# A two-layer H3/MLP training step on one core: four edits to the order of transfers and of one normalisation

## The chip, the core and the metric

The kernel runs on one core of a Trainium2 chip. A core has five engines with queues of their own: TensorE (PE: matmuls; PEld is its loading of weights), VectorE (DVE), ScalarE (ACT), GpSimd (POOL) and SyncE (SP), which issues transfers and does no arithmetic. Transfers (DMAs) are issued by SyncE, ScalarE or GpSimd and carried out by 16 DMA engines that all of these share. [...] The metric is the time of one execution on the device, in microseconds (us), less is better.

## The reference

The program computes a forward pass through four residual blocks and all gradients of it. With S = 2048 positions, D = 448 features and F = 1792 hidden units:

```
x  = A_q
x += A(layernorm(x));  x += B(layernorm(x))      # layer 0
x += A(layernorm(x));  x += B(layernorm(x))      # layer 1

A(q) = q * (irfft(rfft(kv) * rfft(ssm_k)) + kv * ssm_D)
       kv = (k convolved with a filter of 4 taps) * v
B(x) = silu(x @ w1) @ w2
outputs: x, and the gradients for A_q, A_k, A_v, A_shift_k, A_ssm_k, A_ssm_D, B_w1, B_w2
```

The long convolution does not depend on x, so both layers share its result Y. The backward pass of a B block needs, for each position and hidden unit, the slope of silu at the pre-activation, and products of activations and gradients over all positions for the gradients of w1 and w2.

## The kernel before, in words

The program is one Python function that is traced from top to bottom. A planner then puts each engine's instructions in an order of its own: by the order of tracing as a priority, by when it reckons that an instruction's inputs are ready, and by when a buffer comes free. Two calls bind it. `issue_after(x)` puts what is traced inside it behind instruction x on x's engine (order alone, no wait for x to finish); `keep_in_program_order` puts an instruction behind everything traced earlier on its engine. A tile belongs to a pool and a tag, and a tag has a number of buffers; a new tile of a tag can be written only when the oldest one's readers have finished.

The work has these stages, with the times at which they run in the profile of before:

1. **Prefix** (`_ssm_prefix`, 0 to 98 us). It loads k, v, ssm_k and the constants, transposes, and does the long convolution as Fourier transforms made of matmuls. The spectrum of ssm_k is called Ka (in tile Z), the spectrum of kv comes out of A1kv and lies in tile A1K. The loop over two halves h and four groups i does, per step: the short convolution (`conv`, L383), stage 1 of the previous group (`stage1_kv`, L399), in the first half a transposition of a part of Ka's input (`turn`, L365), in the second half two chunks of stage 2 of Ka (`_fft_stage2`, L221, evicted by `cons_ka`). In steps 2 and 3 of the first half `_ln` also normalises the first chunk of positions (tile x0c in, tile na out; ACT L278, DVE L264 to L273). After each two chunks of Ka's spectrum, GpSimd stores them to DRAM (`spec_K`, L413); and it copies them into KB with the two halves of the partitions swapped (`_swap_halves_dma`, L249 and L250). Then stage 2 of kv runs chunk by chunk in `cons_prod`: ScalarE or VectorE evicts the spectrum, GpSimd stores it after each two chunks (`spec_KV`, L448), and VectorE multiplies it by Ka (pa, L451) and by KB (pb, L452) for the inverse transform. The stored spectra are read back in stage 5.
2. **Forward of both layers** (98 to 373 us, `Main.run`, interleaved with layer 1's backward pass). Positions are in four chunks c of 512. `h` multiplies by w1 (tile w1sb, L537) and stores the activations turned (`store_turned`: two transposing DMAs, L503, into the one buffer `turned`, and later a plain store, L504) and, for layer 0, the pre-activations (`DT_d`, L645). `out` multiplies by w2 (tile w2sb). Both weights are loaded right behind the prefix in the tracing (L186 to L189), into the buffers of the prefix's M1sb and v_n.
3. **Backward of layer 1** (228 to 412 us): `ga` multiplies the incoming gradient by w2 transposed (ps_g) and by the slopes (ghT), `gn` multiplies by w1 transposed (ps_n, L740) and goes back through the normalisations on ScalarE and VectorE.
4. **Backward of layer 0** (395 to 517 us): the same with the stored pre-activations, loaded by `load_d` (L769, tile dTl) one chunk ahead and turned into slopes by ScalarE (L614). In `ga`, at steps 3 and 6 of 7, the next half of dTl is loaded, and then a finished half of ghT is turned and stored: for half 0 by `store_turned`, which first issues a store still pending from the half before (`flush`), for half 1 by a plain store (L507). `x_turn` (L674) turns the next chunk's gradient. Jobs of the w2 gradient (`_job`: 16 matmuls ps_d, L904, with an operand tile dstat loaded by L902 or, with transposition, by L900) fill PE in between.
5. **Suffix** (517 to 737 us, `_ssm_suffix`): the backward Fourier transforms, with the jobs of the w2 gradient and then of the w1 gradient (`_gw1`) woven between. `_gw1` makes 14 blocks ft of 128 columns, each of two jobs. ScalarE evicts a block (dout, L966); the first 12 blocks are turned by a transposing DMA (tile do, L941) and stored by two plain DMAs (L933, L934). `store` stores the blocks already turned, and `turn(ft)` is called in the first job of block ft + 1.

The lines that place the store of a turned block and the load of a derivative half:

```
def turn(ft, o):
    if ft < NF - 2:
        store()
        o7 = pool.tile([P, ND, P], BF16, name="do7", tag="do7", bufs=2)
        nc.sync.dma_start_transpose(out=o7[:], in_=o[:])
...
if loads[hh]:
    ld.append(self.load_d(*loads[hh]))
if L == 1 or hh == 0:
    self.store_turned(k.GH_d[L], ghT[hh], c, hh)
```

## Time and profile before

| | |
|---|---|
| median of three runs | 739.4 us (737.02 to 741.23) |
| the profiled execution | 738.77 us, of which the span from the first to the last instruction 736.6 us |
| granted TensorE clock, mean | 0.992 |
| PE, DVE, ACT, POOL busy | 94%, 69%, 58%, 9% of the span |
| bytes moved by DMA | 180.11 MB, mean 245 GB/s |
| issued by SyncE and ScalarE (hardware_dynamic) | 156.34 MB |
| issued by GpSimd (software_dynamic) | 22.65 MB |

A line of the timeline has the start and the duration in us, the engine (SPq: SyncE's queue), the line of the kernel, the operation, the tile written and the tiles read, the number of instructions merged, and in brackets how long the engine stood idle before and what ended that. A transfer's line is the time of its issue; when it lands is another matter. In the rows of 40 slices a digit is the busy share in tenths, 9 for 90% or more.

### The profile page before, as it was taken

How to read it: one execution, taken by the hardware profiler on the slowest of the kernel's cores; microseconds unless marked ns; L12 is line 12 of the kernel's file. 1: busy time of each engine (PE TensorE's matmuls, PEld its weight loads, DVE VectorE, ACT ScalarE, POOL GpSimd, SP SyncE). 2: the span in 40 equal slices, each digit the busy share in tenths (PEclk: the TensorE clock that was granted, in tenths of full speed). 3: DMA queues.
4: the chain of work that ended last, by engine and by line, in shares of the span. 5: the costliest groups of instructions: out<-in, count | busy, mean ns of one | idle time of the engine just before them, and what ended most of it. 6: DMA issues, size and time to landing. Idle time of an engine off the chain costs nothing. (4 is left out here: it accounts for less than half of the span.)

```text
span 736.6 us, 12192 instructions
## 1 busy us (share of the span) xinstructions
PE 690.3 (94%) x4753; PEld 362.6 (49%) x4753; DVE 507.6 (69%) x1059; ACT 424.1 (58%) x539; POOL 62.7 (9%) x111
## 2 busy tenths in 40 slices
PE   6988789999999998999999799999999999999987
PEld 5766533443344443443444334445465767755533
DVE  4878888787743597895958788798224777199423
ACT  4688877766437577487576476763723666531101
POOL 1143221111100002000000000000000000000000
PEclk9999999999999999999999989999999999999999
DMA  9979969999875878979999999997799999899966
GB/s 311 240 179 277 354 212 319 280 290 281 244 153 143 202 158 208 188 205 200 239 223 289 185 348 263 255 270 257 268 252 215 297 322 348 279 275 243 208 144 154
DMA packets 234789, 180.11 MB, mean 245 GB/s; under 512 B 179178, under 2 KB 215598, under 8 KB 233580
## 3 DMA queue, kind: packets, MB, share of 16 engines
q1 hardware_dynamic: 228238, 156.34, 82.4%
q0 software_dynamic: 5872, 22.65, 9.0%
q8 instruction: 37, 0.61, 0.4%
q10 hardware_dynamic: 622, 0.35, 0.3%
q14 instruction: 20, 0.16, 0.1%
HBM read 69.58 MB, written 63.77 MB: 181 GB/s over the span
## 5 line engine op out<-in xcount | busy, mean ns | idle before, releaser
L904 PEld LDWEIGHTS <-dstat 128*128 128x128 bf16 x896 | 85.1, 98 | 80.8 <-DMA dstat<-GP_d 4.4
L537 PE MATMUL ps_h<-nT,w1sb 128*128 128x512 bf16 (+1 forms) x448 | 102.1, 381 | 6.8 <-DVE dT L113 5.2
L537 PE MATMUL ps_g<-gT,w2T 128*128 128x512 bf16 (+1 forms) x448 | 96.0, 381 | 3.2 <-ACT ghp L690 3.1
L740 PE MATMUL ps_n<-w1T,ghT 128*128 128x448 bf16 x448 | 92.6, 360 | 5.0 <-ACT lb_u L742 3.6
L904 PE MATMUL ps_d<-mov,dstat 128*128 128x448 bf16 x448 | 89.5, 352 | 3.5 <-DMA dstat<-GP_d 3.5
L629 ACT ACTIVATE aT<-ps_h 128x1024 bf16<-128x1024 f32 (+1 forms) x64 | 58.4, 916 | 55.2 <-PE ps_h L537 38.3
L658 PE MATMUL ps_o<-w2sb,aT 128*128 128x448 bf16 x448 | 90.1, 353 | 0.0
L113 DVE CAST dT<-ps_h 128x1024 bf16<-128x1024 f32 (+1 forms) x55 | 58.3, 1063 | 27.8 <-ACT aT L629 27.8
L537 PEld LDWEIGHTS <-w1sb 128*128 128x128 bf16 (+1 forms) x448 | 35.9, 96 | 69.7 <-issue 41.2
L740 PEld LDWEIGHTS <-ghT 128*128 128x128 bf16 x448 | 43.5, 99 | 48.6 <-issue 7.7
L537 PEld LDWEIGHTS <-w2T 128*128 128x128 bf16 (+1 forms) x448 | 35.4, 96 | 61.9 <-issue 29.2
L690 ACT CAST ghp<-ps_g 128x1024 bf16<-128x1024 f32 x56 | 55.4, 1007 | 17.1 <-PE ps_g L537 13.1
L658 PEld LDWEIGHTS <-aT 128*128 128x128 bf16 x448 | 42.4, 98 | 42.3 <-issue 3.6
L904 PE MATMUL ps_d<-X,dstat 128*128 128x448 bf16 x224 | 52.2, 353 | 0.0
L904 PE MATMUL ps_d<-GO,dstat 128*128 128x448 bf16 x224 | 50.2, 353 | 0.0
L742 ACT ACTIVATE lb_u<-ps_n,rstd 128x448 f32<-128x448 f32 x32 | 20.2, 633 | 37.0 <-DVE X L727 17.7
L966 ACT CAST dout<-ps_d 128x448 bf16<-128x448 f32 x14 | 7.5, 534 | 51.8 <-PE ps_d L904 43.9
L233 PEld LDWEIGHTS <-pb 128*128 128x128 bf16 x336 | 32.5, 98 | 9.1 <-DVE pb L452 5.7
L614 ACT ACTIVATE dTl<-dTl 128x1024 bf16<-128x1024 bf16 (+1 forms) x32 | 29.8, 944 | 12.0 <-DMA dTl<-DT_d 12.0
L232 PEld LDWEIGHTS <-pa 128*128 128x128 bf16 x336 | 32.8, 98 | 7.2 <-DVE pa L451 4.3
L698 DVE TENSOR_TENSOR ghT<-dT,ghp 128x1024 bf16<-128x1024 bf16 (+1 forms) x32 | 19.8, 621 | 20.4 <-ACT ghp L690 20.3
L659 DVE TENSOR_TENSOR X<-X,ps_o 128x448 bf16<-128x448 bf16 x32 | 19.7, 615 | 16.3 <-PE ps_o L658 16.2
(188 smaller groups left out, 1091.7 us busy)
## 6 DMA issues: line engine op xcount, KB each, us to landing
A_d<-turned SPq DMA_DIRECT2D x12, 896.0 KB, 4.6
GH_d<-turned SPq DMA_DIRECT2D x12, 896.0 KB, 5.1
dstat<-A_d SPq DMA_DIRECT2D x21, 512.0 KB, 5.0
dstat<-GH_d SPq DMA_DIRECT2D x21, 512.0 KB, 4.7
DT_d<-dT SPq DMA_DIRECT2D x8, 896.0 KB, 6.5
dTl<-DT_d SPq DMA_DIRECT2D x8, 896.0 KB, 6.6
spec_K<-Z POOLq DMA_DIRECT2D x7, 512.0 KB, 7.5
KB<-Z POOLq DMA_DIRECT2D x14, 256.0 KB, 12.5
```

The costliest lines, as they stand in the source:

```text
L113: eng.tensor_copy(out, in_)
L232: nc.tensor.matmul(o, lhsT=pa[:, i * P:(i + 1) * P], rhs=k.Gsb[:, ga, :], start=True, stop=False)
L233: nc.tensor.matmul(o, lhsT=pb[:, i * P:(i + 1) * P], rhs=k.Gsb[:, gb, :], start=False, stop=True)
L537: self.nc.tensor.matmul(o, lhsT=w[lo:hi, b, f:f + P], rhs=r, start=(seen[u] == 1), stop=(seen[u] == ND))
L614: self.k.last_slope = self.nc.scalar.activation(s, s, ACT.Derivative_silu)
L629: last = nc.scalar.activation(a, ps[:, 0:n, :], ACT.Silu)
L658: nc.tensor.matmul(po[:, :D], lhsT=aT[ft // 7][0][:, ft % 7, tl * P:(tl + 1) * P], rhs=self.w2sb[:, ft, :], start=(ft == 0), stop=(ft == N ...
L690: k.last_gh = nc.scalar.copy(gh[:], ps[:])
L698: nc.vector.tensor_tensor(out=ghT[hh][:, o:o + len(u), :], in0=dT[hh][1][:, o:o + len(u), :], in1=gh[:, u[0]:u[0] + len(u), :], op=ALU.mult)
L740: mm = nc.tensor.matmul(pn[:, :D], lhsT=ghT[ft // 7][:, ft % 7, tl * P:(tl + 1) * P], rhs=self.w1T[:, ft, :], start=(ft == 0), stop=(ft == ...
L742: last_u = nc.scalar.activation(u0[:], pn[:, :D], ACT.Identity, scale=k.rstd[2 * L + 1][:, t:t + 1], accum_out=cp[:, tl, 0:1])
L904: i = k.nc.tensor.matmul(ps[:, :D], lhsT=st[:, t, :], rhs=mov[:, t, :], start=start and t == 0, stop=stop and t == NT - 1)
```

## The change

Four things are edited, and no arithmetic is:

- In `_gw1`, `turn` issues the transposing DMA of its block first and the stores of the block before it behind that.
- In `ga`, for layer 0 and where a derivative half is loaded, the pending store and both transposing DMAs of `store_turned` are put behind that load.
- In the prefix, the stores of both spectra are issued by SyncE and no longer by GpSimd. The loads of w1 and w2 are traced inside the prefix, ahead of the last three pairs of Ka's chunks.
- In the prefix, the first chunk's normalisation is traced in steps 0 and 1 of the first half and not in steps 2 and 3.

```
     _ssm_prefix(k)
-    k.w1sb = k.wk.tile([P, ND, F], BF16, name="w1sb", tag="WA")
-    nc.sync.dma_start(out=k.w1sb[:, 0:3, :], in_=k.B_w1[0:384].rearrange("(c p) f -> p c f", p=P))
-    nc.sync.dma_start(out=k.w1sb[:, 3, :], in_=k.B_w1[320:448])
-    k.w2sb = k.wk.tile([P, NF, D], BF16, name="w2sb", tag="WB")
-    nc.sync.dma_start(out=k.w2sb[:], in_=k.B_w2.rearrange("(c p) d -> p c d", p=P))
...
-                nc.gpsimd.dma_start(out=k.SPEC_d["K"][:, lo:hi], in_=Ka[:, lo:hi])
+                nc.sync.dma_start(out=k.SPEC_d["K"][:, lo:hi], in_=Ka[:, lo:hi])
...
-                if 4 * h + i in (2, 3):
-                    _ln(k, work, 0, lambda tl: k.x0c0[:, tl, :], 0, k.na0, ((2 * i - 4, 2 * i - 2),), pin=True, store=i == 3)
+                if 4 * h + i in (0, 1):
+                    _ln(k, work, 0, lambda tl: k.x0c0[:, tl, :], 0, k.na0, ((2 * i, 2 * i + 2),), pin=True, store=i == 1)
...
         stage1_kv(*prev)
+        k.w1sb = k.wk.tile([P, ND, F], BF16, name="w1sb", tag="WA")
+        nc.sync.dma_start(out=k.w1sb[:, 0:3, :], in_=k.B_w1[0:384].rearrange("(c p) f -> p c f", p=P))
+        nc.sync.dma_start(out=k.w1sb[:, 3, :], in_=k.B_w1[320:448])
+        k.w2sb = k.wk.tile([P, NF, D], BF16, name="w2sb", tag="WB")
+        nc.sync.dma_start(out=k.w2sb[:], in_=k.B_w2.rearrange("(c p) d -> p c d", p=P))
...
-                nc.gpsimd.dma_start(out=k.SPEC_d["KV"][:, (ci - 1) * 1024:(ci + 1) * 1024], in_=Zf[:, (ci - 1) * 1024:(ci + 1) * 1024])
+                nc.sync.dma_start(out=k.SPEC_d["KV"][:, (ci - 1) * 1024:(ci + 1) * 1024], in_=Zf[:, (ci - 1) * 1024:(ci + 1) * 1024])
...
                 if L == 1 or hh == 0:
-                    self.store_turned(k.GH_d[L], ghT[hh], c, hh)
+                    with self.tc.issue_after(k.d_load.ins) if L == 0 and loads[hh] else ExitStack():
+                        self.store_turned(k.GH_d[L], ghT[hh], c, hh)
...
         if ft < NF - 2:
-            store()
             o7 = pool.tile([P, ND, P], BF16, name="do7", tag="do7", bufs=2)
-            nc.sync.dma_start_transpose(out=o7[:], in_=o[:])
+            with k.tc.issue_after(nc.sync.dma_start_transpose(out=o7[:], in_=o[:]).ins):
+                store()
```

## The prediction

> **What bounds the kernel now.** I read the page first: TensorE (PE) is the bound.

> ```profile
> PE 690.3 (94%) x4753; PEld 362.6 (49%) x4753; DVE 507.6 (69%) x1059; ACT 424.1 (58%) x539; POOL 62.7 (9%) x111
> DMA  9979969999875878979999999997799999899966
> ```

> PE is free for only 46.3 us of the 736.6 us span, and the DMA engines are nearly full for most of it. So an edit gains only where it closes a hole in PE or a stretch at half clock. I therefore went through the timeline in windows, looked for those holes near the edited lines, and then asked the view of waits who ended each. There are four places.

> *Place 1, the end of the w1 gradient.* SyncE's queue (SPq), then PE, both from the timeline (start, duration, ..., idle before and who ended it):

> ```profile
> 695.95 1.22 SPq L941 DMA_TRANSPOSE do<-dout  x1
> 701.94 0.40 SPq L933 DMA_DIRECT2D out_dram<-do  x1
> 703.00 2.26 SPq L900 DMA_TRANSPOSE dstat<-GP_d  x1
> ...
> 707.58 6.23 PE L904 MATMUL ps_d<-mov,dstat 128*128 128x448 bf16 x32 [1.36 <-DMA dstat<-GP_d]
> 715.97 10.77 PE L904 MATMUL ps_d<-mov,dstat 128*128 128x448 bf16 x56 [2.16 <-DMA dstat<-GP_d]
> ```

> The planner put the store of a turned block (L933) right behind that block's own transpose (L941). SyncE stands still from 697.17 to 701.94 until the transpose lands, the load of the next operand stands behind it, and PE starves twice: 1.36 + 2.16 = 3.5 us.

> *Place 2, the first chunk of the layer-0 backward pass.* SyncE, ScalarE and PE:

> ```profile
> 410.37 2.83 SPq L503 DMA_TRANSPOSE turned<-ghT  x1
> 413.24 0.58 SPq L769 DMA_DIRECT2D dTl<-DT_d  x1
> ...
> 421.23 1.06 ACT L614 ACTIVATE dTl<-dTl 128x1024 bf16<-128x1024 bf16 x1 [7.37 <-DMA dTl<-DT_d]
> ...
> 416.15 2.81 PE L740 MATMUL ps_n<-w1T,ghT 128*128 128x448 bf16 x14
> 422.95 5.38 PE L740 MATMUL ps_n<-w1T,ghT 128*128 128x448 bf16 x14 [3.61 <-ACT lb_u L742]
> ```

> The derivative input is issued behind a transpose and lands at 413.24 + 8.0. ScalarE waits 7.37 us for it, with the reading of a PSUM bank queued behind. PE idles 3.61 us, and then runs the same 14 matmuls in 5.38 instead of 2.81 us, because the clock has dropped. Together 3.61 + 2.57 = 6.2 us.

> *Place 3, the prefix, where the first chunk's normalisation stands.*

> ```profile
> 36.83 1.74 PE L383 MATMUL ps_cv<-KB 112*128 112x112 bf16 x32
> 39.17 1.03 PE L221 MATMUL ps_s<-Z,Gsb 128*128 128x512 bf16 x4
> 42.37 2.97 PE L383 MATMUL ps_cv<-KB 112*128 112x112 bf16 x32 [2.17 <-ACT A1kv L111]
> 46.33 1.03 PE L221 MATMUL ps_s<-Z,Gsb 128*128 128x512 bf16 x4
> ...
> 40.06 1.41 ACT L278 ACTIVATE na<-x0c,ln_nmr,rstd 128x448 bf16<-128x448 bf16 x2 [0.50 <-DVE ln_nmr L273]
> ```

> From one set of stage-2 matmuls to the next it is 46.33 - 39.17 = 7.2 us; the next two steps take 3.4 us each (49.70, 53.10). ScalarE does the normalisation (1.41 us, again at 43.19) ahead of the evictions that PE waits for, and after the hole the convolution takes 2.97 instead of 1.74 us. Excess: 3.8 us.

> *Place 4, the swapped spectrum KB.*

> ```profile
> 71.89 0.57 POOL L413 DMA_DIRECT2D spec_K<-Z  x1 [0.85 <-DMA KB<-Z]
> 75.50 0.52 POOL L250 DMA_DIRECT2D KB<-Z  x1 [1.25 <-DMA KB<-Z]
> ...
> 84.75 0.69 DVE L452 TENSOR_TENSOR pb<-A1K,KB 128x1024 bf16<-128x1024 bf16 x1 [1.76 <-DMA KB<-Z]
> ```

> From 64 us on each transfer of GpSimd (POOL) starts just as the one eight places ahead of it lands, so the stores of the spectrum take places from the swaps. VectorE, busy for nearly all of 68 to 82 us, then stands 1.76 us for a swap that was issued at 70.53 and took 14.0 us.

> [...] at 42.37 a hole of 2.17 us was enough, and the 2.16 us hole at 713.8 was not, so I count the clock only where the trace shows it.

> **The change part by part.**

> *Stores of w1 blocks.* The transpose of block n+1 now precedes the store of block n, whose own transpose is then some 6 us old (two jobs of 16 matmuls, 3.03 us each), against landing times of 2.5 to 7.6 us. Nothing is added: same 12 transposes and 24 stores. SyncE loses its waits there (21.7 us over 9 stores), and the operand load for 707.58 can issue at about 697.2, landing with its 4.5 us at 702, 4 us ahead of need. Bounds: 0 (if SyncE's issue time of 5 to 7 us per 6.06 us pair of jobs binds by itself) to 3.5. I take 3.5, since the slots come free four jobs ahead. Next late would be a transpose waiting for the store two blocks back; that store has 6 us to land in.

> *Derivative inputs.* Three chunks, L769 ahead of two transposes (L503). In the first, the slot is free when ghT's half is done, about 407.5, so the load issues some 5.5 us sooner and lands near 413 (shortest seen 5.7 us), when ScalarE wants it. The price: the pending store of the previous turned half (405.42, 4.9 us) is queued behind the load too, and the transposes wait for its buffer. They start near 414.5, not 410.37; but the transfers up to the next gT are the same, so later landings stay about where they are. That caps the gain: grad_out (GO) lands at 429.17 + 11.8 = 441.0 for a first use at 444.83, 3.9 us of slack; the next derivative lands at 429.2 for 433.54, 4.3; VectorE's chain, which restarts at 422.94, could restart at 418.5, 4.4. So of 6.2 us I take 3.9. In the second chunk the load must wait for its slot until about 439.3 and holds back a transpose that issued at 434.39, but transfers were backed up until 441 anyway: 0. In the third it gains nothing on PE. Bounds: -2 (a transpose or GO later by the length of one load, which shows nowhere now) to 6.2.

> *Normalisation two steps sooner.* Same instructions. The excess of 3.8 us goes. The steps at 27 to 36 us, paced by PE at 3.2 us, receive 3.7 us of VectorE work (bn_stats 0.6 each and small ones) and 2.8 of ScalarE. Before each eviction there ScalarE idles 1.0 to 1.8 us and VectorE 0.8 to 1.1, so most fits; in-order queues will delay some evictions. I charge 1.2 and take 2.6. Bounds -1 to 3.8. Its input was issued at 10.20 and took 13.8 us, so it is there at 24.

> *Spectra on SyncE.* 14 issues of 0.54 us leave GpSimd, and 14 places free up. The swaps then issue several us sooner and DVE's 1.76 us goes: 1.7. Bounds 0 to 2.5 (with 0.69 at 67.45). SyncE is idle from 58.9 to 89.7, so the 14 issues cost nothing there; the spectra are first read at 524.8. Queued behind them are the x0 loads (89.74, 7.0 us to land), wanted at 102.18: if the stores back up, that slack of 5 us, shrunk by the 4.3 won, goes first.

> *w1 and w2 loads traced sooner.* They issued at 54.16 to 57.40 and were first used at 102.5. They only have to stay ahead of the stores: 0.

> Sum: 3.5 + 3.9 + 2.6 + 1.7 = 11.7. The profiled execution took 738.77 around its span of 736.6; minus 11.7 it is 727.1. The median of the runs is 739.4, 0.6 above it: **727.7 us**.

> **Rivals.**
> (a) Layer 0 is fed by the DMA engines, busy through all of 410 to 490 (share 1.06): the stall moves to GO or the next derivative. For: slacks of only about 4 us. Then 3.5 + 2.6 + 1.7: 731.6.
> (b) The prefix gains nothing: evictions now wait behind the normalisation in steps paced by PE, or x0 is late. With the other two parts in half: about 735.5.
> (c) All holes close with no new one: 3.5 + 6.2 + 3.8 + 2.5 = 16, 723.4.
> (d) Slower: the load, first in SyncE's queue, waits for its slot while transposes, stores and the next operand stand behind it, and each of the three chunks stalls as the first does now. Two new stalls of 6.2 us and the old one kept cost 12.4 against 7.8 won: 744. It decides once ScalarE's waits pass about 4 us per chunk. Against: the slot is freed by the very multiplication whose result the transposes need.
> (e) The change doesn't do what it says, because the planner times everything else anew: within 0.5%, near 738.

> **How the numbers follow.** Forecast 0.58, (a) 0.17, (b) 0.07, (c) 0.08, (d) 0.05, (e) 0.05. The likeliest case spans 724 to 731.5; with (a) and part of (c) the range is 722 to 734.5. Half a per cent (3.7 us) is about what a measurement here can tell: faster 0.88, same 0.07, slower 0.05.

> **What would show it.** Right: L933 behind the next L941 with no wait for do<-dout, and no PE hole at dstat<-GP_d; L769 ahead of both L503 and the 7.37 us wait nearly gone; no half clock near 42 or 422; no pb wait for KB. Wrong: ScalarE waiting for dTl in the second or third chunk, PE waiting for GO, holes of 1 us in steps at 27 to 36 us, or x0c late at 98.

## The result, and the profile after

The changed kernel took 728.6 us (median of four runs, 727.79 to 731.37) against 739.8 before (four runs; the first three gave 739.4): a ratio of 0.987, 95% interval 0.984 to 0.990. The forecast was 727.7. Measured again later, beside 27 executions of the kernel before, it was 729.8 (six executions) against 736.3: 0.991, interval 0.988 to 0.994. Both put the time inside the forecast range, and both intervals lie below 1; but the gain was 11 us the first time and 6.6 the second, and the difference is what the experiments had to explain.

The page of the kernel after, engines and DMA share:

```profile
PE 689.2 (95%) x4753; PEld 361.7 (50%) x4753; DVE 507.4 (70%) x1059; ACT 424.0 (58%) x539; POOL 55.0 (8%) x97
DMA  9969959999976877878989999999699898999994
```

TensorE's free time fell from 46.3 to 727.5 - 689.2 = 38.3 us, its work stayed, and GpSimd lost the 14 stores. The timeline of the same kernel at the four places (start, duration, queue or engine, ..., idle before and who ended it):

```profile
33.28 1.41 ACT L273 ACTIVATE na<-x0c,ln_nmr,rstd 128x448 bf16<-128x448 bf16 x2 [1.27 <-DVE ln_nmr L268]
...
35.53 1.73 PE L378 MATMUL ps_cv<-KB 112*128 112x112 bf16 x32 [1.19 <-ACT ks L380]
38.01 0.93 PE L394 MATMUL ps_s<-kvt,M1sb 128*128 128x224 bf16 x8 [0.74 <-DVE Z L113]
...
69.94 0.52 POOL L245 DMA_DIRECT2D KB<-Z  x1 [0.55 <-DMA KB<-Z]
...
82.25 0.69 DVE L452 TENSOR_TENSOR pb<-A1K,KB 128x1024 bf16<-128x1024 bf16 x1
...
407.48 0.32 SPq L770 DMA_DIRECT2D dTl<-DT_d  x1
...
413.71 1.04 ACT L614 ACTIVATE dTl<-dTl 128x1024 bf16<-128x1024 bf16 x1
...
419.13 2.81 PE L741 MATMUL ps_n<-w1T,ghT 128*128 128x448 bf16 x14
...
425.76 1.17 SPq L871 DMA_DIRECT2D GO<-in_grad_out_dram  x1
427.04 8.70 SPq L674 DMA_TRANSPOSE gT<-X  x1
...
700.04 17.95 PE L905 MATMUL ps_d<-mov,dstat 128*128 128x448 bf16 x94
...
700.88 1.21 SPq L941 DMA_TRANSPOSE do<-dout  x1
702.19 0.52 SPq L934 DMA_DIRECT2D out_dram<-do  x1
...
703.34 2.49 SPq L901 DMA_TRANSPOSE dstat<-GP_d  x1
```

- *The end.* The store (L934) follows the next block's transpose without a stop, the operand's load (L901) follows at once, and 94 matmuls run from 700.04 to 717.99 with no hole.
- *Layer 0, first chunk.* The derivative load (L770) goes at 407.48, ScalarE has its input at 413.71 without a wait, and the 14 matmuls that stood 3.61 us and ran 5.38 now come unbroken in 2.81.
- *Spectrum.* The last swap is issued at 69.94 (one was still to come at 75.50 before), and the pb of VectorE that waited 1.76 us before, now at 82.25, waits for nothing, like all others.
- *Prefix.* The holes at 42 us are gone, but the normalisation at 33.28 now stands ahead of ScalarE's eviction, and TensorE stands 1.19 and 0.74 us at 35 and 38.

By differences of start times between the two profiled executions: tail -3.87, last matmuls -0.37, layer 0 -5.11 and +0.29, convolution -1.24, spectrum -1.73, a later start +0.59, between the first ps_y and layer 0 +2.38, where a half-clock stretch came (granted clock 0.50 from 98.89 to 105.71 us; 1.00 there before), elsewhere -0.05; together -9.1, the difference of the spans.

### The profile page after: what moved, and what is told of

Same layout as the page of the kernel before. It is cut to its first block, busy times and chain, and to the rows that moved or that the text cites. A ratio compares the mean times of both kernels' runs of the same rounds, so it can differ in the third digit from the quotient of the medians.

```text
span 727.5 us, 12191 instructions
## 1 busy us (share of the span) xinstructions
PE 689.2 (95%) x4753; PEld 361.7 (50%) x4753; DVE 507.4 (70%) x1059; ACT 424.0 (58%) x539; POOL 55.0 (8%) x97
## 5 line engine op out<-in xcount | busy, mean ns | idle before, releaser
L537 PE MATMUL ps_h<-nT,w1sb 128*128 128x512 bf16 (+1 forms) x448 | 104.7, 389 | 6.6 <-DVE dT L113 5.1
L741 PE MATMUL ps_n<-w1T,ghT 128*128 128x448 bf16 x448 | 90.2, 353 | 2.1 <-DVE ghT L698 2.0
L614 ACT ACTIVATE dTl<-dTl 128x1024 bf16<-128x1024 bf16 (+1 forms) x32 | 29.8, 943 | 6.6 <-DMA dTl<-DT_d 6.6
```

What stands on the lines that cost most here:

```text
L537: self.nc.tensor.matmul(o, lhsT=w[lo:hi, b, f:f + P], rhs=r, start=(seen[u] == 1), stop=(seen[u] == ND))
L614: self.k.last_slope = self.nc.scalar.activation(s, s, ACT.Derivative_silu)
L741: mm = nc.tensor.matmul(pn[:, :D], lhsT=ghT[ft // 7][:, ft % 7, tl * P:(tl + 1) * P], rhs=self.w1T[:, ft, :], start=(ft == 0), stop=(ft == ...
```

## The experiments

Each was timed against the kernel before on its own chip. A single part is worth less than the spread of the runs, so I also measured stages in each trace, from the start of one set of matmuls to that of another, which keeps a gain apart from what happens elsewhere. "Convolution" runs from the first ps_cv matmul to the 225th, "spectrum" on to the first ps_y, "chunk 1" from the 253rd ps_n to the 337th, "rest of layer 0" on to the first ps_gK, "tail" from the first ps_sk to the first ps_dt.

### The four parts alone, on the kernel before

*w1 stores:*

```diff
-            store()
             o7 = pool.tile(...)
-            nc.sync.dma_start_transpose(out=o7[:], in_=o[:])
+            with k.tc.issue_after(nc.sync.dma_start_transpose(out=o7[:], in_=o[:]).ins):
+                store()
```

> The kernel before with the w1 block stores alone put behind the next block's transpose. Theory (four independent gains): the two PE holes at dstat<-GP_d, 1.36 and 2.16 us, go, and the end comes 3.5 to 3.9 us sooner, with nothing changed before 690 us. Rival (the holes closed because the earlier stages ran ahead and the DMA engines were freer by then): under 1.5 us, one of the two holes stays.

Ratio 0.9966 (0.9949 to 0.9982), medians 733.1 against 735.7, so 2.6 us, with an interval of 1.3 to 3.8. Tail: 34.66 us, in this run and in all seven others with this part 34.65 to 34.81; in the six without it 36.81 to 39.09, mean 38.02. That is 3.4 us on average, 3.9 from the profiled execution that I predicted from. The rival falls: both holes go without the earlier parts, as the timeline of this kernel shows.

```profile
706.02 17.95 PE L904 MATMUL ps_d<-mov,dstat 128*128 128x448 bf16 x94
```

*Derivative loads:*

```diff
-                    self.store_turned(k.GH_d[L], ghT[hh], c, hh)
+                    with self.tc.issue_after(k.d_load.ins) if L == 0 and loads[hh] else ExitStack():
+                        self.store_turned(k.GH_d[L], ghT[hh], c, hh)
```

> The kernel before with the layer-0 derivative loads alone put ahead of the transposes. My recorded cap: 3.9 us. Theory after the result: about 5 us, since GO and the next derivative load move up too, so the 3.61 us hole and the half clock behind it (2.57 us) both go, and 1 us comes back with a wait further on. Rival (it needs the prefix to run ahead): under 3 us.

Ratio 0.9997 (0.9976 to 1.0018): nothing. That is the rival's number, but not for its reason. The profiled execution was the longest of its 22 (741.2 us against a median of 735.9), so it is read for its places, not for its length. Chunk 1 is as after (47.57 us), so the move works alone; but the rest of layer 0 is 165.04 instead of 159.46, with a wait of TensorE for an operand (dstat<-A_d, 4.83 us) that the kernel before doesn't have. Neither theory nor cap foresaw that; "The third chunk" below follows it.

*Normalisation:*

```diff
-                if 4 * h + i in (2, 3):
-                    _ln(..., ((2 * i - 4, 2 * i - 2),), pin=True, store=i == 3)
+                if 4 * h + i in (0, 1):
+                    _ln(..., ((2 * i, 2 * i + 2),), pin=True, store=i == 1)
```

> The kernel before with the first chunk's normalisation alone moved to steps 0 and 1. Theory: 1.2 us sooner at 47 us (the 3.8 us excess goes, holes of 1.2 and 0.7 us come at 35 to 38 us), and that much or less at the end. Recorded: 2.6. Rival (a stall only changed its place): 0 to 0.5 at 47 us, or slower.

Ratio 0.9998 (0.9983 to 1.0014). The convolution takes 25.12 us, 1.24 less than before, and the spectrum stage gives it back: 42.49 instead of 41.45. VectorE of this kernel, in the timeline:

```profile
84.79 0.69 DVE L452 TENSOR_TENSOR pb<-A1K,KB 128x1024 bf16<-128x1024 bf16 x1 [2.68 <-DMA KB<-Z]
```

It arrives sooner at the same late swap and waits 2.68 instead of 1.76 us. With the swaps as they were, the normalisation's place is worth nothing that these times can tell (0.2 us at the first ps_y).

*Spectra on SyncE, w1 and w2 loads moved:*

```diff
-                nc.gpsimd.dma_start(out=k.SPEC_d["K"][:, lo:hi], in_=Ka[:, lo:hi])
+                nc.sync.dma_start(out=k.SPEC_d["K"][:, lo:hi], in_=Ka[:, lo:hi])
...
-                nc.gpsimd.dma_start(out=k.SPEC_d["KV"][:, ...], in_=Zf[:, ...])
+                nc.sync.dma_start(out=k.SPEC_d["KV"][:, ...], in_=Zf[:, ...])
```

with the five lines of the w1 and w2 loads moved into the prefix as in the change.

> The kernel before with the spectra stored by SyncE and the w1 and w2 loads moved, nothing else. Theory: VectorE's wait of 1.76 us for KB goes and the first ps_y matmul comes 1.7 us sooner, kept to the end. Rival (the prefix's end is paced by something else and the wait shows up there): 0 to 0.5.

Ratio 0.9981 (0.9962 to 1.0000). The spectrum stage takes 39.71 us, against 41.45 before: 1.7, as forecast. It is 39.71 or 39.72 in the five other profiles with this part in which the normalisation is not put on VectorE. The 0.37 us at the end comes with this part too, which nobody forecast: from the first ps_dt to the end of the span it is 9.69 to 9.71 us in the eight profiles with the spectra on SyncE and 10.06 to 10.22 in the six without. Why, no run here shows.

By their ratios the four parts alone sum to 4.3 us, and the change measured whole gives 6.6 (below). About 1 us of the difference is the normalisation, which needs the spectra moved; the rest is within the intervals.

### Does the gain hang on the execution?

The same file as the changed kernel.

> The changed kernel once more, on one chip with the next three and the kernel before. Theory: its gain does not hang on the chip, 9 to 11 us, and its executions show the half clock near 100 us again. Rival (single parts summed to only some 4 us, and each profiled execution loses a different number of half-clock windows): the gain is 5 to 8 us here, and part of the 11 measured first was the clock and the chip.

0.9911 (0.9880 to 0.9942): 6.6 us, the rival's 5 to 8. This time the profiled execution (span 725.1 us) had no half clock at all before the end (mean granted clock 0.998). The view of windows, cut into steps of 3.41 us (in the first profile 98.89 and 105.71 us, where the granted clock changed, bound two of them; columns: window, its length, TensorE busy, granted clock, DMA share, GB/s), of the kernel after, first profile:

```profile
95.48:98.89 3.41, 1.71 (x19) 1.00 0.82 330
98.89:102.30 3.41, 2.52 (x10) 0.50 0.39 148
102.30:105.71 3.41, 3.41 (x11) 0.50 0.00 0
```

and of the same kernel in its second:

```profile
94.75:98.16 3.41, 1.88 (x15) 1.00 0.92 370
98.16:101.58 3.42, 2.27 (x16) 1.00 0.40 153
101.58:104.99 3.41, 3.34 (x18) 1.00 0.01 4
```

The holes at this place are the same (1.43, 0.27 and 0.9 to 1.0 us). Only the steps fell otherwise: one step held TensorE busy for 1.71 us and the clock was halved for the next two; here the emptiest held 1.88 and it was not. What filled the step differs too: 1.14 of the 1.71 us were transposes on TensorE (matmuls with the identity, ps_t<-ident), against 0.71 of the 1.88. Over all 14 profiles the stage from the first ps_y to the 253rd ps_n takes 323.6 to 324.0 us in the five without half clock near 100 us and 325.1 to 327.2 in the nine with it, 2.4 more on average.

At the hole that place 2 was priced from, a half clock is a matter of the execution as well. Kernel before:

```profile
418.07:421.48 3.41, 1.27 (x7) 1.00 1.37 117
421.48:424.90 3.42, 1.95 (x6) 0.50 1.32 161
```

and the kernel with the normalisation alone moved, whose code there is unchanged and whose wait for lb_u was 1.33 us:

```profile
419.09:422.50 3.41, 2.63 (x14) 1.00 1.27 251
422.50:425.91 3.41, 2.85 (x16) 1.00 1.09 204
```

So chunk 1 took 52.73 us in the profile that I predicted from, but 50.42, 49.91, 49.62 and 49.55 in four other kernels with the same code, against 47.6 with the load moved (48.64 in one of nine). In that one execution ScalarE had the load late enough for a hole of 3.61 us, against 0.98 to 1.85 in the other four, and the hole left TensorE busy for only 1.27 us of one step of the clock.

### The third chunk

In the changed kernel, the load moved in the first chunk only; SyncE's order differs only in the third, where one transpose stands ahead of the load again:

```diff
-                    with self.tc.issue_after(k.d_load.ins) if L == 0 and loads[hh] else ExitStack():
+                    with self.tc.issue_after(k.d_load.ins) if L == 0 and c == 0 and loads[hh] else ExitStack():
```

> The changed kernel with the derivative load ahead of the transposes in the first layer-0 chunk only; SyncE's order differs from the changed kernel's only in the third chunk, where one transpose goes ahead of the load again. Theory: the third chunk gains nothing, and having both transposes behind the load makes the operand loads that follow late (a wait of 4.83 us for dstat<-A_d in the run with this part alone, 0.76 in the changed kernel): 0.5 to 1 us faster than the changed kernel in the median, and no wait for A_d near 505 us. Rival: the order in the third chunk does nothing, within 0.3 us of the changed kernel.

0.9900 (0.9872 to 0.9928), median 728.65 against 729.77 for the changed kernel beside it: the right direction, not separable by times. The trace is clearer: no wait for A_d; the rest of layer 0 takes 159.73 us.

The same single-chunk edit alone, on the kernel before:

> The kernel before with the derivative load ahead of the transposes in the first layer-0 chunk only. Theory: the gain of the first chunk (2 to 3 us without the clock, 5 with it) stays to the end since the late operand near 507 us does not come: 2 to 3.5 us faster than before in the median. Rival (the derivative part gains nothing on the average, since the half clock behind its hole was that one execution's): within 1 us of before, as with all three chunks.

0.9981 (0.9962 to 0.9999), 1.8 us by medians where all three chunks gave 0: just under the 2 that the theory asked for, and above the rival's 1. The two intervals overlap, so that the third chunk takes the gain back is read from the traces and from the spread: the 22 times of the kernel with all three chunks have a standard deviation of 3.3 us, against 2.2 here and 2.1 for the kernel before. Chunk 1 took 47.57 us, the rest 159.96.

Over all the traces, the rest of layer 0 takes 159.46 to 159.75 us in the five kernels with the old order everywhere, 159.71 to 159.96 in the three with only the first chunk moved, and 159.47, 159.75, 160.17, 162.30, 165.04 and 165.52 in the six with all three. So the third chunk costs nothing in some executions and 6 us in others. The loss goes with the time for which the two transposes of that chunk (L503) hold SyncE: 8.8, 11.4, 11.7, 12.6, 13.6 and 14.8 us in the six profiles, and TensorE's wait for A_d there is 0, 0.76, 1.65, 2.19, 4.83 and 4.51 us.

### The normalisation on VectorE

On the changed kernel (the four instructions are then not counted in the balance, which shifts a few later choices):

```diff
-                    _ln(..., ((2 * i, 2 * i + 2),), pin=True, store=i == 1)
+                    _ln(..., ((2 * i, 2 * i + 2),), pin=True, eng=nc.vector, store=i == 1)
```

> The changed kernel with the early normalisation's four scale-and-shift instructions on VectorE instead of where the balance put them. Theory: the new PE hole of 1.19 us at ks goes, since ScalarE's queue no longer has 1.41 us ahead of the eviction, while VectorE's 0.3 us each lengthen the wait at Z: 0.5 to 1 us sooner at the convolution's end than the changed kernel, of which what reaches the first ps_y matmul is less. Rival (the prefix's end is paced by the swaps into KB): nothing at ps_y.

0.9879 (0.9848 to 0.9911). Convolution 23.87 us instead of 25.11, and the spectrum stage 39.19 instead of 39.71, so all of it arrives: 1.8 us at ps_y, more than the 0.5 to 1 expected. The rival falls. Whether the 0.5 us of the spectrum stage is the normalisation's or that of the shifted choices isn't shown. But in the profiled execution, 4.5 us went at the third chunk. Its timeline there, SyncE's queue and TensorE:

```profile
457.03 14.77 SPq L503 DMA_TRANSPOSE turned<-ghT  x2
...
480.91 8.95 SPq L503 DMA_TRANSPOSE turned<-ghT  x2
494.41 0.53 SPq L504 DMA_DIRECT2D GH_d<-turned  x1
...
495.74 2.51 SPq L903 DMA_DIRECT2D dstat<-A_d  x2
...
503.69 1.67 PE L905 MATMUL ps_d<-GO,dstat 128*128 128x448 bf16 x4 [4.51 <-DMA dstat<-A_d]
505.16 4.59 PE L741 MATMUL ps_n<-w1T,ghT 128*128 128x448 bf16 x14
```

Both transposes behind the derivative load keep SyncE for 14.8 us, and what is queued behind them follows late; the next pair takes another 8.95, the store of its tile (L504) waits until it has landed, at 494.40, and the operand's load behind that goes at 495.74 for a use at 499.2. Behind the hole the 14 matmuls take 4.59 instead of 2.81 us.

### Both together

The last two edits on the changed kernel.

> The changed kernel with the normalisation's four scale-and-shift instructions on VectorE and the derivative load moved in the first layer-0 chunk only. Theory: the 1.7 us that the first gained at ps_y stays, since the wait of 4.5 us for dstat<-A_d that took it back near 500 us is gone with the old order in the third chunk: 11.5 to 13 us faster than before, 2 to 4 faster than the changed kernel. Rival (the wait for A_d comes from the execution, not from the order in the third chunk): it shows again, and the gain is that of the changed kernel.

```profile
455.60 3.86 SPq L503 DMA_TRANSPOSE turned<-ghT  x1
459.56 0.95 SPq L770 DMA_DIRECT2D dTl<-DT_d  x1
460.56 1.64 SPq L503 DMA_TRANSPOSE turned<-ghT  x1
...
479.30 6.24 SPq L503 DMA_TRANSPOSE turned<-ghT  x2
487.79 0.53 SPq L504 DMA_DIRECT2D GH_d<-turned  x1
...
489.13 5.38 SPq L903 DMA_DIRECT2D dstat<-A_d  x2
...
498.15 1.68 PE L905 MATMUL ps_d<-X,dstat 128*128 128x448 bf16 x8
499.67 0.92 PE L905 MATMUL ps_d<-GO,dstat 128*128 128x448 bf16 x4
```

With one transpose ahead of the load SyncE is held for 3.9 + 1.6 us at that place, the operand is there, and TensorE doesn't stop. The profiled execution has the shortest span of all, 723.3 us, with no half clock before the end (mean granted clock 0.999). The times do not carry that far: 0.9879 (0.9853 to 0.9906), 728.59 against 736.73, 8.1 us; the other five spans were at 726.3 to 727.7. That is under the 11.5 expected, and its interval overlaps the changed kernel's.

### Undoing one part of the change

Normalisation back in steps 2 and 3 (the hunk of that part reversed):

> The changed kernel with the normalisation put back to steps 2 and 3. Theory: with the swaps no longer pacing the prefix's end, the normalisation's place is worth at ps_y what it is worth at the convolution's end, 1.1 to 1.2 us, against the 0.2 that came through alone; so 1 to 1.2 us slower than the changed kernel. Rival: nothing comes through here either, ps_y within 0.3 us of the changed kernel.

Counted from the first ps_cv matmul, ps_y comes after 66.10 us, 1.27 later than in the changed kernel's second profile: what the part moves at the convolution's end (26.38 against 25.11) now arrives whole, of which about 0.6 may be the clock's, an estimate from two other kernels with the old place, whose convolutions took 25.78 and 25.79 us (mean granted clock 0.991 in this profile, 0.998 in the changed kernel's). The whole kernel is at 0.9927 (0.9896 to 0.9958).

Spectra and weight loads back (those two hunks reversed):

> The changed kernel with the spectra back on GpSimd and the w1 and w2 loads back at their old place. Theory: ps_y 2.7 to 2.9 us later than in the changed kernel (1.9 from the spectra alone, and the normalisation's 0.9 that their waits hide again), VectorE waiting for KB near 84 us. Rival (the parts simply add): 1.7 to 1.9 us.

ps_y 67.24 us after the first ps_cv against 64.83: 2.41 later, between the two expectations, with VectorE waiting 2.24 us for KB; 0.9931 (0.9909 to 0.9954). More than 1.7 is what a hidden gain of the normalisation would give; but the mean granted clock was 0.993 here and 0.998 there, so this one isn't shown.

Spectra moved, weight loads left at their old place, on the kernel before:

> The kernel before with the spectra stored by SyncE and the w1 and w2 loads left where they were; SyncE then issues the last two w1 loads behind four stores of the first spectrum and two of the second. Theory: ps_y about 1.9 us sooner, as with the loads moved, and the w1 loads land near 95 us, still ahead of their first use: nothing lost. Rival (they become late): the first ps_h matmul waits for w1sb, by more than 1 us.

0.9970 (0.9955 to 0.9985), spectrum stage 39.71 us: the same as with the loads moved. The w1 loads landed at 85.8 and 89.9, ahead of their use at 100.1, and the first ps_h matmul waited for nT, not for w1. Moving the weight loads is worth nothing here.

## Why the prediction was right, and where it wasn't

The time was right and so were the sign, the four places and the waits that end there. The size of the gain was not: two terms of the sum were mis-sized, and a loss and the draw of the clock were missing. That 727.7 met 728.6 so closely is partly luck. The forecast gain of 11.7 us, a ratio of 0.984, lies inside the interval of the first measurement and outside that of the second, beside which the kernel before was 3.5 us faster.

- **Stores, 3.5.** Right: 3.4 on average, 3.9 between the profiles. The named rests of doubt (SyncE's issue time, a slot not free) did not appear.
- **Derivative load, 3.9 of 6.2.** Failed twice. The cap ("later landings stay about where they are") was wrong: the planner also moved the next derivative load and GO ahead of the turning of X (gT<-X at 427.04 behind GO at 425.76; before, at 416.26 and 429.17), so GO landed at 435.9 instead of 441.0, and between the two profiles 5.1 us were kept in the first chunk. But the 6.2 that it was cut from was one execution's: the same place costs 1.9 to 2.8 us in the four other kernels that have it, against the 3.9 forecast. And "in the third it gains nothing on PE" missed a loss: the third chunk takes back 0 to 6 us, because SyncE's queue behind the pair of transposes carries the operand loads of the w2 gradient. The prediction had asked of the moved load what stands behind it, but answered for ScalarE's input only. Rival (d) was near: it had work, the next operand too, held up behind the reordered load. SyncE does stand before that load, for 0.5 to 1.9 us in the six profiles with this order, but the larger delay is that of the transposes, and it comes in one chunk of three.
- **Normalisation, 2.6.** The 3.8 us excess again contained a half clock (0.50 from 42.60 to 46.02 us; 2.97 instead of 1.74 for one convolution step). The charge of 1.2 for delayed evictions was too low: holes of 1.19 and 0.74 us came in the steps named for it. At the convolution's end 1.0 us remains on average, 1.24 between the first two profiles, and 0.7 against the two kernels with the old place that took 25.78 and 25.79 us. That even this arrives is owed to the spectrum part: alone, it was worth nothing, since VectorE ran into the late swap. These two parts do not simply add.
- **Spectra, 1.7.** Right in size, in place and in kind (the wait for KB gone; before, GpSimd's issues at 64.49, 66.57 and 75.50 us came 0.6, 0.2 and 0.3 us after the landing of the one eight places ahead), and the weight loads rightly counted as 0.
- **The clock.** Counting it "only where the trace shows it" was the weak step: a trace shows it for one execution, and the changed kernel's two executions differ (0.50 from 98.89 to 105.71 us in one, 1.00 at the same holes in the other). So half-clock time in one profile is a draw: the one of before drew the holes at 42 and 418 us (its matmuls took 2.97 instead of 1.74 and 5.38 instead of 2.81 us, 1.2 and 2.6 longer) and not the one near 100 us, which nine of the other thirteen profiles drew, the first of after too (2.4).

Put together from the averages over traces: tail 3.4, chunk 1 50.45 - 47.69 = 2.8 less about 1.9 in the rest of layer 0 (mean of five profiles with all three chunks, without the long one; 2.5 with it), convolution 1.0, spectrum 1.7, the end 0.4: 7.4 us (6.8 with the long one), near the 6.6 of the second measurement. The first one's 11 us had a kernel before at 739.8, 3 to 4 us above its medians in the later sets (735.7, 736.3, 736.7). Whether that is the chip or the draw of few executions, no run here tells.

What stays open: why the pair of transposes in the third chunk is served in 8.8 to 14.8 us in executions with the same order, and so which share of executions pays for it. That TensorE's operand is late because of them rests on the queue's timeline, on the six waits that grow with the pair's time, and on the three kernels without that order, none of which waits; with one profile of each kernel that is strong but not proof. What slows the transposes is not shown.

## What to carry to other kernels

Price a hole from several executions, or from the wait alone, and never from matmuls that ran at half clock behind it: the same three holes near 100 us (2.6 to 2.7 together) came with half clock in one execution of the changed kernel and without in another. When an issue is moved forward on a queue, list every later transfer on that queue with its first use, chunk by chunk: a reorder that helps the first chunk of a loop can hurt its third, and then it may belong in the first alone (here the times of the two could not be told apart, only the traces). Two parts that feed the same join, here VectorE's product of spectrum and swap, have to be measured together, since one of them alone may show nothing.

## What the runs showed of the hardware

Of the full-speed steps on these grids from 11 us on and up to the last 8 us, three were followed by half clock. TensorE was busy in them for 1.24 us (before, 39.19 to 42.60), 1.27 us (before, 418.07 to 421.48) and 1.71 us (after, 95.48 to 98.89). All others had 1.83 us or more, and full speed followed; the emptiest were 1.83 (before, from 83.56), 1.92 (before, from 97.22) and 2.03 us (after, from 409.50). The two holes of nearly equal length in the profile of before, 2.17 us at 42.37 and 2.16 us at 713.8, lie in steps that differ by this count: 1.24 us of matmuls from 39.19 on, and then half clock; 2.19 us from 711.62 on, and full clock still. I had expected the length of a hole to decide; in these two profiles the busy time of a step parts the cases and that length doesn't.

Whether transposes on TensorE count in this like other matmuls is not shown: they made up 1.14 of the 1.71 us that half clock followed, and 0.71 of the 1.88 us (second profile of the changed kernel, from 94.75) that it did not.
